# Mask read-back of a fused sparse-attention and FFN kernel: four SP transfers to 32 partitions, or two Pool transfers to 128

## The chip, the cores and the metric

The kernel runs on one core of a Trainium2 chip. The metric is the device time of one execution in microseconds, the median of several runs. Engines are named as in the profile: PE (TensorE), PEld (its weight loads), DVE (VectorE), ACT (ScalarE), POOL (GpSimd) and SP (SyncE, which here only issues DMAs). Each of SP and POOL feeds a DMA queue of its own; both queues are served by the same 16 DMA engines.

## The reference

Two operations in a row. First, attention over 4 sequences ("batches"), 8 heads, 768 positions and 64 channels, in which each query sees only 6 chunks of 32 keys; then a feed-forward block on the result.

```
k_min, k_max = min, max of each chunk of 32 keys
ub     = sum over channels of max(q * k_min, q * k_max)     # bound per query and chunk
ub     = -1e9 where the chunk lies in the query's future
sel    = the 6 chunks with the highest ub, for each query
scores = q k^T / 8, -1e9 where not (selected and key <= query)
x      = softmax(scores) v                                   # [3072, 512]
out    = relu(x w_in)^2 w_out                                # 512 -> 2048 -> 512
```

## The kernel before

The work is cut into 16 head pairs (4 batches of 4 pairs) and 5 FFN blocks. The first 128 queries of every sequence can see only the first four chunks, so they need no selection: they are computed first for all batches, and are the first FFN block. The other 640 queries (5 tiles of 128) of each batch follow, batch by batch, and each batch is an FFN block when its attention result `x` is complete.

For batches 0 and 1 the selection goes into the score product itself: 24 extra rows of the matmul operands add a large negative number where a chunk isn't selected. For batches 2 and 3 (the last two sequences, pairs 8 to 15) it goes another way, in `stage_a_turned`:

1. Keys and queries come turned, by DMA transposes on SP (`kt`, `qt`). DVE reduces the keys to chunk maxima and minima (`kr`, two reductions a pair, L666), halves the queries (`qp`, `qm`, L688), PE computes the bounds (`ub`, L656 and L658), DVE masks them (`ubm`, L680), finds the highest eight (`m`, MAX8, L651) and writes ones and zeros, scaled to a huge number and zero, into `selb` (L785).
2. SP turns `selb` by a DMA transpose into `sT` and writes that to a buffer in device memory, `seen` (L802).
3. SP reads `seen` back into `mask`, [128 keys, 2 heads, 20 units, 128 queries], repeating each row of `seen` for the 32 keys of its chunk (L806). A unit is a pair of a query tile and a key tile. `seen` holds 4 groups of 40 rows, one group for each chunk within a key tile, so four DMAs are issued, one for each group of 32 partitions, 328 kB each.
4. POOL makes the five diagonal blocks of the mask causal (`mask<-mask`, L835, five instructions a pair).
5. In `stage_b_turned`, PE computes scores (`ps`, L913), ACT the exponentials (`e`, L951), DVE takes the minimum of `e` and `mask` (L953, ten instructions a pair), PE multiplies by the values (`av`, L946), and DVE normalises into `x` (reciprocal L638, product L640).

The mask buffers come from a pool of two (`set`), which the extra-row operands of the first two batches use before them. So a pair's mask can be fetched only when the pair two before it has had its last minimum.

An FFN block needs `x` turned; for batches 1 to 3 that is five DMA transposes on SP (`xT<-x`, L414). PE's `ph` (L1009) is the first FFN product, ACT or DVE apply the ReLU (`ht`, L1016 and L1018), DVE squares (`h`, L1027), PE's `py` (L1040) is the second product, ACT copies it to `ob` (L300), and SP stores it (L1053).

The order of instructions on every engine is written by a planner, `Plan`, before anything runs. Each operation has its candidate engines with a cost, a due time, needs and tiles; `Plan.order` starts, on the engine that is free first, the operation with the earliest due time. Due times come from a table of fitted numbers, `P`: `lead` (how far ahead each pair's selection is due), `due` and `rate` (the FFN blocks), `loads` and `later` (the order of loads), `shift` (changes to single operations) and some more. DMAs are costed by `packets`, through a small model of the two queues, `Transfers`. An operation with `packets` and without `turns` is a load on POOL; loads keep a given order among themselves:

```
if op.packets and not op.turns and op is not self.loads[len(landed)]:
    continue
```

Once planned, each engine runs its instructions in that order, and a DMA's wait holds up all that its issuing engine has behind it.

Of the kernel before, what the change touches and what calls it, by code (L numbers as in the profile page):

```python
# [81 lines left out]
class Plan:  # L82
# [19 lines left out]
        self.loads = []  # L102

    def op(self, where, due, fn, needs=(), tiles=(), packets=0, turns=False,
           late=0.0, rows=128):
        op = Op(where, due, fn, [n for n in needs if n is not None],
                [t for t in tiles if t is not None], packets, turns)
        for t in op.tiles:
            t.users.append(op)
        op.late = late  # L110
        op.rows = rows
        op.number = -1 if packets and not turns else len(self.ops) - len(self.loads)
        self.ops.append(op)
        if packets and not turns:
            self.loads.append(op)
        return op

    def order(self):
        free = {e: 0.7 for e in ("PE", "ACT", "DVE", "POOL", "SP")}
        slots = {tag: [(0.0, i) for i in range(n)] for tag, n in self.slots.items()}  # L120
        waiting = {}
        count = {}
        for op in self.ops:
            for t in op.tiles:
                t.left = len(t.users)
            count[op] = len(op.needs)
            for n in op.needs:
                waiting.setdefault(n, []).append(op)
        ready = [op for op in self.ops if not count[op]]
        landed, done = [], []  # L130
        rows = 128
        dma = Transfers()
        while ready:
            found = []
            for op in ready:
                if op.packets and not op.turns and op is not self.loads[len(landed)]:
                    continue
                at = 0.0
                new = {}
                for t in op.tiles:  # L140
                    if not t.held:
                        new[t.tag] = new.get(t.tag, 0) + 1
                for tag, n in new.items():
                    at = max(at, sorted(slots[tag])[n - 1][0]
                             if n <= len(slots[tag]) else self.NEVER)
                if at == self.NEVER:
                    continue
                if op.packets and not op.turns and len(landed) >= 8:
                    at = max(at, landed[-8].end)
                for engine, cost in op.where.items():  # L150
                    st = max(at, free[engine])
                    for n in op.needs:
                        same = n.engine == engine and not n.packets
                        lag = (0.0 if engine == "PE" else self.BUSY) if same                             else self.HAND_OVER[n.engine]
                        st = max(st, n.end + lag)
                    for t in op.tiles:
                        if t.psum:
                            for e, end in t.last.items():
                                if e != engine and "PE" not in (e, engine):
                                    st = max(st, end + self.HAND_OVER[e])  # L160
                    found.append((st, op, engine, cost))
            assert found, "nothing can start"
            first = min(found, key=lambda f: (f[0], f[1].number))
            st, op, engine, cost = min(
                (f for f in found if f[2] == first[2] and f[0] <= first[0] + self.wait),
                key=lambda f: (round(f[1].due, 6), f[0], f[1].number))
            ready.remove(op)
            if engine == "PE":
                op.fill = 0
                fresh = [t for t in op.tiles if t.psum]  # L170
                if st < self.FILL and fresh and not any(t.held for t in fresh):
                    room = max([free[engine]] + [min(slots[t.tag])[0] for t in fresh])
                    op.fill = max(0, int((st - room - 0.3) / 0.216))
                if st < self.WARM:
                    cost *= 2
                if op.rows != rows:
                    cost += self.SWITCH
                rows = op.rows
            op.engine, op.start, op.end = engine, st, st + cost
            free[engine] = op.end  # L180
            if op.packets:
                dma.add(op)
                if not op.turns:
                    landed.append(op)
            for t in op.tiles:
                if not t.held:
                    t.held = True
                    slot = min(slots[t.tag])
                    slots[t.tag].remove(slot)
                    t.slot = slot[1]  # L190
                t.last[engine] = max(t.last.get(engine, 0.0), op.end)
                t.left -= 1
                if not t.left:
                    slots[t.tag].append(
                        (max(u.end + self.HAND_OVER[u.engine] for u in t.users),
                         t.slot))
            for n in waiting.get(op, ()):
                count[n] -= 1
                if not count[n]:
                    ready.append(n)  # L200
            done.append(op)
        assert len(done) == len(self.ops), "operations left"
        return sorted(done, key=lambda op: op.start)
# [12 lines left out]
def kernel(  # L216
# [9 lines left out]
    nc = tc.nc  # L226
# [17 lines left out]
    QC = 128 * NS  # L244
    VW = 80
    NSET = 4
    P = dict(lead=[-23.68, 210.01, 152.21, 144.05, -31.58, 102.41, 35.34, 55.13,
             115.99, 34.19, 31.08, 95.55, 110.01, 67.89, 4.75, 130.36], f_due=[381.13,
             -1344.18, -1072.84, -487.16], sp='K0 Q0 K1 Q1', rows=[-2152.97, -1713.16,
             -252.64, -1284.21, 1259.55, -368.8, -2131.49, -296.06], after=1,  # L250
             up_due=-58.884, up_rate=11.985, half=4, due=[-23.83, -165.81, -133.7,
             266.6], rate=[4.21, 8.73, 10.38, 24.63], va=22.291, vm=16.1, ra=-3.615,
             h2=-15.315, later='q1 k1 v1 k2 q2 v3 q3 v2 k3', shift={522: 9.76, 1364:
# [9 lines left out]
             1171: -9.73, 528: -4.83, 1419: -7.53, 1620: 4.17}, p0=-4855.279,  # L263
             wait=0.012, xt=(1, 2, 3), ub='ff', tp=1, vm2=3.232, va2=7.671,
             loads='V1 V0 Q3 K3 Q2 K2 i0 V2 k0 V3 q0 i1 k1 v2 q1 i2 v0 '
             'i3 k2 q2 o0 v1 o2 o1 k3 o3 v3 q3')

    nc.scalar.preload_act_table_set("natural_log_exp_and_others")

# [482 lines left out]
    NU = len(UNITS)  # L752
# [3 lines left out]
    written, placed = [], []  # L756

    def stage_a_turned(p):
        b, hp = divmod(p, NP)
        s = p % NSET  # L760
        t0 = HALVES * p - P["lead"][p]
        op = plan.op
        kT, qT = turned["k", b], turned["q", b]
        qp, qm = buffer("qp", [128, QC]), buffer("qm", [128, QC])
        ub = buffer(P["ub"], [128, NS, 2, NC], F32, name="ub")
        sT = buffer("st", [128, 2, 128], name="sT")
        seen = buffer("seen", [2 * 128, 128], name="seen")
# [23 lines left out]
        def pick(i0, i1):  # L791
            for i in range(i0, i1):
# [5 lines left out]
               for i, n in ((0, 3), (3, 2))]  # L798
# [4 lines left out]
            out=seen.tile.rearrange("(x r) j -> r x j", r=128), in_=sT.tile),  # L803
            [t] + written[-1:], [sT, seen], packets=300, turns=True, late=1.0)
        written.append(w)
        spread = [op({"SP": 0.45}, t0 + 25 + g, lambda _, g=g: nc.sync.dma_start(  # L806
            out=mask[32 * g:32 * g + 32].rearrange("c h u j -> c (h u j)"),
            in_=seen[2 * NU * g:2 * NU * (g + 1)].rearrange(
                "r j -> (r j)").unsqueeze(0).to_broadcast([32, 2 * NU * 128])),
            [w] + placed[-1:], [seen, mask], packets=930, turns=True, late=0.5) for g in range(4)]  # L810
        placed.append(spread[0])
        prepared[p, "mask"] = [op({"POOL": 0.37}, t0 + 30 + t, lambda _, t=t:
                                  causal("POOL", mask[:, :, FIRST[t] + t + 1], 2),
# [247 lines left out]
    for b in range(B):  # L1061
        due = P["f_due"][b]
# [18 lines left out]
    for b in range(B):  # L1081
# [28 lines left out]
        if last:  # L1110
            down(NS - 1, 0, 384)
            down(NS - 1, 384)
    computed = [op for op in plan.ops if op.turns or not op.packets]
    for i, change in P["shift"].items():
        computed[i].due += change
    with tc.manual_schedule():
# [31 lines left out]
```

## Time and profile before

| | |
|---|---|
| median of 3 runs | 274.06 us (273.2 to 274.55) |
| profiled execution | 274.56 us, span 272.7 us, granted clock 0.987 |
| PE, PEld busy | 252.5 us (93%), 159.1 us (58%) |
| DVE, ACT, POOL busy | 203.5, 181.6, 111.3 us (75, 67, 41%) |
| POOL queue | 75088 packets, 13.11 MB, 64.1% of 16 engines |
| SP queue | 33904 packets, 23.73 MB, 41.4% of 16 engines |
| mask read-back | 32 DMAs of 320 KB, median 5.9 us from issue to landing |

A row of a timeline reads: start, duration (us), engine, line, operation, output<-input, count, and in brackets the idle time of that engine before it and what ended it. A row of the chain reads: start, duration, engine, tile, line, count. In rows of groups, the numbers behind the bar are busy us, mean ns of one, and idle time before with what ended it. KB there is 1024 bytes.

### The profile page before, as it was taken

How to read it: one execution, taken by the hardware profiler on the slowest of the kernel's cores; microseconds unless marked ns; L12 is line 12 of the kernel's file. 1: busy time of each engine (PE TensorE's matmuls, PEld its weight loads, DVE VectorE, ACT ScalarE, POOL GpSimd, SP SyncE). 2: the span in 40 equal slices, each digit the busy share in tenths (PEclk: the TensorE clock that was granted, in tenths of full speed). 3: DMA queues.
4: the chain of work that ended last, by engine and by line, in shares of the span. 5: the costliest groups of instructions: out<-in, count | busy, mean ns of one | idle time of the engine just before them, and what ended most of it. 6: DMA issues, size and time to landing. Idle time of an engine off the chain costs nothing.

```text
span 272.7 us, 6942 instructions
## 1 busy us (share of the span) xinstructions
PE 252.5 (93%) x2519; PEld 159.1 (58%) x2543; DVE 203.5 (75%) x760; ACT 181.6 (67%) x361; POOL 111.3 (41%) x186
## 2 busy tenths in 40 slices
PE   7888999999999999997699989986999999999995
PEld 2566466656677556663486645543776654775443
DVE  7449999887999999994489999986989840355000
ACT  6767898747996988983287745774887741487111
POOL 7979887799179685620303030432003400000000
PEclk9999999999999999999599999999999999999999
DMA  9999999999999999969694829779497025100022
GB/s 157 153 173 159 174 192 189 98 160 199 125 126 183 135 176 144 103 129 191 132 252 83 199 52 229 181 196 198 127 216 151 0 60 154 77 2 0 38 79 78
DMA packets 109026, 37.29 MB, mean 137 GB/s; under 512 B 100672, under 2 KB 105024, under 8 KB 107968
## 3 DMA queue, kind: packets, MB, share of 16 engines
q0 software_dynamic: 75088, 13.11, 64.1%
q1 hardware_dynamic: 33904, 23.73, 41.4%
q8 instruction: 20, 0.33, 0.5%
q14 instruction: 14, 0.11, 0.2%
HBM read 37.75 MB, written 6.82 MB: 163 GB/s over the span
## 4 chain that ended last, share of the span: by engine, by line
PE 46%; DVE 34%; DMA 9%; POOL 5%; issue 2%; ACT 1%; SPq 0%; DVEq 0%; POOLq 0%; ACTq 0%
PE py L1040 19%; PE ph L1009 17%; DVE kr L666 7%; DVE h L1027 5%; DMA xT<-x 4%; DVE selb L785 4%; DVE m L651 3%; DVE ht L1018 3%; DVE e L953 3%; PE ps L855 3%; DMA mask<-seen 3%; DMA qn<-in_q_dram 2%; PE av L946 2%; PE av L867 2%; PE ps L913 2%
## 5 line engine op out<-in xcount | busy, mean ns | idle before, releaser
L1009 PE MATMUL ph<-xT,w_in_sb 128*128 128x256 bf16 (+2 forms) x592 | 97.3, 307 | 8.5 <-DMA xT<-x 5.9
L1040 PE MATMUL py<-w_out_sb,h 128*128 128x512 bf16 (+2 forms) x376 | 89.1, 372 | 2.2 <-DVE ubm L680 0.7
L1009 PEld LDWEIGHTS <-w_in_sb 128*128 128x128 bf16 x592 | 55.5, 98 | 35.4 <-DMA xT<-x 6.5
L1016 ACT ACTIVATE ht<-ph 128x384 bf16<-128x384 f32 (+2 forms) x115 | 52.2, 455 | 26.8 <-PE ph L1009 21.3
L1027 DVE TENSOR_TENSOR h<-ht 128x256 bf16<-128x256 bf16 (+2 forms) x148 | 48.0, 336 | 12.0 <-ACT ht L1016 9.4
L1040 PEld LDWEIGHTS <-h 128*128 128x128 bf16 x400 | 35.9, 98 | 34.8 <-issue 1.5
L835 POOL TENSOR_SCALAR_AFFINE_SELECT mask<-mask 128x256 bf16<-128x256 bf16 x40 | 19.1, 514 | 76.8 <-DMA mask<-seen 45.8
L951 ACT ACTIVATE e<-ps 128x512 bf16<-128x512 f32 x80 | 42.9, 603 | 9.9 <-PE ps L913 9.2
L879 ACT ACTIVATE e<-ps 128x512 bf16<-128x512 f32 x80 | 43.5, 611 | 4.5 <-PE ps L855 4.1
L300 ACT COPY ob<-py 128x512 f32<-128x512 f32 (+2 forms) x25 | 14.2, 569 | 37.7 <-PE py L1040 37.3
L953 DVE TENSOR_TENSOR e<-e,mask 128x512 bf16<-128x512 bf16 x80 | 33.0, 437 | 7.5 <-POOL mask L835 6.8
L1018 DVE TENSOR_SCALAR ht<-ph 128x256 bf16<-128x256 f32 (+2 forms) x33 | 15.9, 481 | 15.2 <-PE ph L1009 15.1
L855 PE MATMUL ps<-kqc 88*128 88x128 bf16 (+2 forms) x160 | 25.9, 272 | 0.4
L835 POOL TENSOR_SCALAR_AFFINE_SELECT e<-e 128x128 bf16<-128x128 bf16 (+1 forms) x50 | 17.3, 360 | 16.5 <-ACT e L879 16.3
L946 PEld LDWEIGHTS <-e 128*128 128x128 bf16 x320 | 15.4, 100 | 9.1 <-DVE e L953 2.2
L640 DVE TENSOR_TENSOR x<-av,rc 128x320 bf16<-128x320 f32 (+1 forms) x40 | 18.4, 469 | 0.3
L946 PE MATMUL av<-vn,e 128*128 128x65 bf16 x240 | 17.9, 196 | 0.4 <-DVE e L953 0.2
L855 PEld LDWEIGHTS <-kqc 88*128 88x128 bf16 x160 | 13.6, 97 | 7.3 <-issue 1.1
L867 PEld LDWEIGHTS <-e 128*128 128x128 bf16 x320 | 13.8, 97 | 3.3 <-POOL e L835 0.3
L651 DVE MAX8 m<-ubm 128x8 f32<-128x24 f32 x160 | 15.2, 164 | 0.1
L666 DVE TENSOR_REDUCE kr<-kt 128x24 bf16<-128x768 bf16 x16 | 14.8, 938 | 0.0
L666 DVE TENSOR_REDUCE kr<-kT 128x24 bf16<-128x768 bf16 x16 | 14.8, 948 | 0.1
(96 smaller groups left out, 312.4 us busy)
## 6 DMA issues: line engine op xcount, KB each, us to landing
mask<-seen SPq DMA_DIRECT2D x32, 320.0 KB, 5.9
out_dram<-ob SPq DMA_DIRECT2D x23, 256.0 KB, 3.2
w_in_sb<-in_moe_w_in_dram POOLq DMA_DIRECT2D x4, 512.0 KB, 7.7
w_out_sb<-in_moe_w_out_dram POOLq DMA_DIRECT2D x4, 512.0 KB, 8.5
vn<-in_v_dram POOLq DMA_DIRECT2D x15, 128.0 KB, 6.1
nt<-in_k_dram POOLq DMA_DIRECT2D x10, 128.0 KB, 7.5
nt<-in_q_dram POOLq DMA_DIRECT2D x10, 128.0 KB, 6.6
kn<-in_k_dram POOLq DMA_DIRECT2D x8, 80.0 KB, 7.3
```

The costliest lines, as they stand in the source:

```text
L666: nc.vector.tensor_reduce(split(kr[:, mm]), by_chunk(view(kT)), axis=AX.X, op=f), got, [kT, kr])
L835: nc.gpsimd.affine_select(out=e, in_=e, compare_op=ALU.is_ge, fill=0.0, base=0, channel_multiplier=-1, pattern=[[0, n], [1, 128]])
L855: nc.tensor.matmul(ps[:, 128 * c:128 * (c + nt)], lhsT=kqs(slice(0, KC), s, hh)[:, 128 * j:128 * (j + 1)], rhs=qss(slice(0, KC), s, hh)[:, ...
L879: nc.scalar.activation(e.tile, ps.tile, ACT.Exp, scale=scale), [sc], [ps, e])
L946: nc.tensor.matmul(av[:, t - 1], lhsT=e[:, 128 * c:128 * (c + 1)], rhs=value_tile(b, h, j), start=(i == 0 and c == 0), stop=(i == NB - 1), ...
L951: done = plan.op({"ACT": 0.48}, due + 0.5, lambda _: nc.scalar.activation(e.tile, ps.tile, ACT.Exp, scale=scale), [sc], [ps, e])
L953: done = plan.op({"DVE": 0.335}, due + P["vm2"], lambda _: nc.vector.tensor_tensor(e.tile, e.tile, masks[p][:, hh, 4 * i:4 * i + 4].rearrange(
L1009: nc.tensor.matmul(ph.tile, lhsT=w_in_sb[:, ki, 128 * f:128 * (f + 1)], rhs=xT[:, c0 // 128:c1 // 128, ki], start=(ki == 0), stop=(ki == N ...
L1016: nc.scalar.activation(ht.tile, ph.tile, ACT.Relu)
L1018: nc.vector.tensor_scalar_max(ht.tile, ph.tile, 0.0)
L1027: {"DVE": 0.067 + w / 1920}, at[0] + P["h2"], lambda _: nc.vector.tensor_mul(h2[f][:, c0:c1], ht.tile, ht.tile), [op], [ht, h2[f]])))
L1040: nc.tensor.matmul(py.tile, lhsT=h2[f][:, 128 * t:128 * (t + 1)], rhs=w_out_sb[:, f, c0:c1], start=(f == 0), stop=(f == NFI - 1))
```

## The change

The read-back of the mask moves from SP to POOL and is cut by head instead of by group of partitions: two DMAs a pair, each for one head and all 128 partitions, 655 kB each. The source is viewed as 4 groups, each repeated 32 times. The new DMAs are marked `free`: they aren't in the loads' fixed order, but count as transfers of POOL's queue. The table `P` is fitted anew, so the order of instructions changes on every engine; in `later`, batch 3's keys now stand before its queries.

```
     def op(self, where, due, fn, needs=(), tiles=(), packets=0, turns=False,
-           late=0.0, rows=128):
+           late=0.0, rows=128, free=False):
...
-        op.number = -1 if packets and not turns else len(self.ops) - len(self.loads)
+        op.load = bool(packets) and not turns and not free
+        op.number = -1 if op.load else len(self.ops) - len(self.loads)
...
-                if op.packets and not op.turns and op is not self.loads[len(landed)]:
+                if op.load and op is not self.loads[loads]:
                     continue
...
                 if not op.turns:
                     landed.append(op)
+                    loads += op.load
...
-    P = dict(lead=[-23.68, 210.01, 152.21, 144.05, -31.58, 102.41, 35.34, 55.13,
+    P = dict(lead=[-18.56, 229.84, 152.55, 102.48, -28.79, 99.16, 39.06, 55.0, 124.03,
...
-             h2=-15.315, later='q1 k1 v1 k2 q2 v3 q3 v2 k3', shift={522: 9.76, 1364:
+             h2=-3.478, later='q1 k1 v1 k2 v3 q2 k3 v2 q3', shift={1461: -2.33, 615:
...
-             loads='V1 V0 Q3 K3 Q2 K2 i0 V2 k0 V3 q0 i1 k1 v2 q1 i2 v0 '
-             'i3 k2 q2 o0 v1 o2 o1 k3 o3 v3 q3')
+             loads='V0 K3 Q2 V1 K2 Q3 i0 V2 k0 V3 q0 i1 k1 v2 q1 i2 v0 '
+             'i3 k2 q2 o0 v1 o2 k3 o1 o3 v3 q3')
...
-        spread = [op({"SP": 0.45}, t0 + 25 + g, lambda _, g=g: nc.sync.dma_start(
-            out=mask[32 * g:32 * g + 32].rearrange("c h u j -> c (h u j)"),
-            in_=seen[2 * NU * g:2 * NU * (g + 1)].rearrange(
-                "r j -> (r j)").unsqueeze(0).to_broadcast([32, 2 * NU * 128])),
-            [w] + placed[-1:], [seen, mask], packets=930, turns=True, late=0.5) for g in range(4)]
+
+        def spread_rows(hh):
+            rows = seen[0:8 * NU].rearrange("(g h u) j -> g h (u j)", g=4, h=2)
+            nc.gpsimd.dma_start(
+                out=mask[:, hh].rearrange("c u j -> c (u j)"),
+                in_=rows[:, hh].unsqueeze(1).to_broadcast([4, 32, NU * 128]))
+
+        spread = [op({"POOL": 0.80}, t0 + 25 + hh, lambda _, hh=hh: spread_rows(hh),
+                     [w] + placed[-1:], [seen, mask], packets=2000, free=True, late=0.3)
+                  for hh in range(2)]
```

In the order that the planner writes now, SP has 32 DMAs fewer and POOL 16 more. POOL has nothing of batches 0 and 1 left when the first of them is reached; from there on its instructions are the mask DMAs and the forty causal selects alone.

More of the change, by code (lines that the diff above doesn't have):

```diff
@@ L111, in op @@
         op.rows = rows
-        op.number = -1 if packets and not turns else len(self.ops) - len(self.loads)
+        op.load = bool(packets) and not turns and not free
+        op.number = -1 if op.load else len(self.ops) - len(self.loads)
         self.ops.append(op)
-        if packets and not turns:
+        if op.load:
             self.loads.append(op)
@@ L129, in order @@
         ready = [op for op in self.ops if not count[op]]
-        landed, done = [], []
+        landed, done, loads = [], [], 0
         rows = 128
@@ L246 @@
     NSET = 4
-    P = dict(lead=[-23.68, 210.01, 152.21, 144.05, -31.58, 102.41, 35.34, 55.13,
[L248 to L252, printed above, removed]
-             h2=-15.315, later='q1 k1 v1 k2 q2 v3 q3 v2 k3', shift={522: 9.76, 1364:
[9 rows of a table removed]
-             1171: -9.73, 528: -4.83, 1419: -7.53, 1620: 4.17}, p0=-4855.279,
-             wait=0.012, xt=(1, 2, 3), ub='ff', tp=1, vm2=3.232, va2=7.671,
-             loads='V1 V0 Q3 K3 Q2 K2 i0 V2 k0 V3 q0 i1 k1 v2 q1 i2 v0 '
-             'i3 k2 q2 o0 v1 o2 o1 k3 o3 v3 q3')
+    P = dict(lead=[-18.56, 229.84, 152.55, 102.48, -28.79, 99.16, 39.06, 55.0, 124.03,
+             40.34, 7.99, 96.78, 112.44, 66.15, 16.87, 125.31], f_due=[-61.33,
+             -1388.83, -1240.75, -707.33], sp='K0 Q0 K1 Q1', rows=[-1131.22, -1431.25,
+             109.16, 501.8, -517.91, 1199.14, -3841.51, 427.48], after=1,
+             up_due=-63.179, up_rate=9.427, half=4, due=[-24.24, -119.06, -171.27,
+             87.42], rate=[4.2, 9.11, 10.54, 36.48], va=15.226, vm=4.436, ra=2.591,
+             h2=-3.478, later='q1 k1 v1 k2 v3 q2 k3 v2 q3', shift={1461: -2.33, 615:
[9 rows of a table added]
+             -10.62, 1597: 9.23, 1075: 10.49, 1343: -1.75}, p0=-9815.44, wait=0.009,
+             xt=(1, 2, 3), ub='ff', tp=1, vm2=6.919, va2=10.415,
+             loads='V0 K3 Q2 V1 K2 Q3 i0 V2 k0 V3 q0 i1 k1 v2 q1 i2 v0 '
+             'i3 k2 q2 o0 v1 o2 k3 o1 o3 v3 q3')
     nc.scalar.preload_act_table_set("natural_log_exp_and_others")
@@ L1112 @@
             down(NS - 1, 384)
-    computed = [op for op in plan.ops if op.turns or not op.packets]
+    computed = [op for op in plan.ops if not op.load]
     for i, change in P["shift"].items():
```

18 rows, old and new, of the table h2 are left out of this document.

## The prediction

> **What bounds the kernel now.** I read the page's busy shares and its chain that ended last, then that chain in order of time around the change, the waits, each queue's timeline there, and the busy time by stage. The time is 274.56 us for the profiled execution, whose span is 272.7 us; 1.9 us lie outside the span. The median of the three runs is 274.06 us, so a sum made on 274.56 loses 0.5 us at the end.
>
> ```profile
> PE 252.5 (93%) x2519; PEld 159.1 (58%) x2543; DVE 203.5 (75%) x760; ACT 181.6 (67%) x361; POOL 111.3 (41%) x186
> ```
> ```profile
> 125.50 6.04 DMA xT<-x
> 131.59 1.03 PE ph L1009 x4
> ...
> 173.39 6.88 DMA mask<-seen
> 180.57 0.41 POOL mask L835
> ...
> 181.53 1.45 DVE e L953 x3
> ...
> 183.98 5.64 DMA xT<-x
> 189.76 0.60 PE ph L1009 x4
> 190.48 0.86 PE py L1040 x4
> ```
>
> PE has little air: 272.7 - 252.5 = 20.2 us. A change can give back only what PE loses, so I look where that is. The chain shows two transposes by DMA, of batch 1's and batch 2's attention result (`xT<-x`), and a mask between them.
>
> ```profile
> 120.00:136.00 16.00, 12.00 (x114) 6.66 (x116) 8.54 (x44) 6.14 (x13) 2.21 (x5) 0.81 0.87 152
> 136.00:152.00 16.00, 15.80 (x154) 11.08 (x152) 15.26 (x45) 12.51 (x29) 2.25 (x5) 0.97 0.67 167
> 152.00:168.00 16.00, 14.46 (x172) 8.88 (x173) 16.00 (x81) 8.55 (x18) 2.15 (x5) 1.00 0.69 151
> 168.00:184.00 16.00, 14.60 (x196) 8.35 (x197) 14.35 (x49) 11.58 (x23) 5.41 (x10) 1.00 0.79 194
> 184.00:200.00 16.00, 13.66 (x196) 9.85 (x195) 12.86 (x56) 10.59 (x25) 1.84 (x5) 1.00 0.82 171
> 131.60:136.20 4.60, 4.38 (x29) 2.89 (x31) 2.45 (x8) 1.72 (x4) 1.13 (x3) 0.50 0.51 104
> ```
>
> The columns are the stretch, its length, busy time of PE, PEld, DVE, ACT, POOL, then the granted clock, DMA share and GB/s. PE is idle 4.0 us in the first stage, 0.2 + 1.5 + 1.4 in the next three, 2.3 in the fifth: 9.5 us in all. The last line is the second bill for the first stop: after it PE runs at half clock for 4.6 us, 2.3 us lost. DVE is full from 136 to 168, and idle just before:
>
> ```profile
> 131.59 1.03 PE L1009 MATMUL ph<-xT,w_in_sb 128*128 128x256 bf16 x4 [3.69 <-DMA xT<-x]
> ```
> ```profile
> 130.97 1.14 DVE L953 TENSOR_TENSOR e<-e,mask 128x512 bf16<-128x512 bf16 x2 [5.24 <-POOL mask L835]
> ```
> ```profile
> 120.88 1.98 SPq L806 DMA_DIRECT2D mask<-seen  x4
> 122.96 1.17 SPq L414 DMA_TRANSPOSE sT<-selb  x1
> 124.22 8.35 SPq L414 DMA_TRANSPOSE xT<-x  x5
> 180.58 2.07 SPq L806 DMA_DIRECT2D mask<-seen  x4
> 182.75 6.90 SPq L414 DMA_TRANSPOSE xT<-x  x5
> 222.63 2.50 SPq L414 DMA_TRANSPOSE xT<-x  x2
> ```
>
> This is the mechanism. Each time four mask DMAs go out on SP's queue, the five transposes that PE wants next are issued right behind them: 1.67 us each (8.35 / 5) and 1.38 (6.90 / 5), against 1.25 (2.50 / 2) where no mask is ahead. Their landing suffers too:
>
> ```profile
> DMA to landing us min/median/max: 2.4/2.7/6.8
> ```
> ```profile
> DMA to landing us min/median/max: 3.7/5.9/10.4
> ```
>
> The first line is `xT`, the second `mask`. PE's first FFN block needs two transposes. Without a mask ahead the second would be issued at 124.22 + 1.25 and land 2.7 later, at 128.2, not 131.5.
>
> **The change: the mask transfers.** 32 issues leave SP, 16 come to POOL; 10.5 MB move either way. What a transfer of the new form costs the trace does not show; two stretches bound it.
>
> ```profile
> 198.00:209.00 11.00, 11.00 (x134) 7.36 (x132) 9.80 (x30) 8.68 (x20) 2.22 (x5) 1.00 1.02 214
> 253.00:273.00 20.00, 16.41 (x92) 8.23 (x90) 0.07 (x1) 3.08 (x6) 0.00 (x0) 1.00 0.18 67
> ```
>
> From 198 to 209 only masks are on the move, into 32 partitions each: 214 GB/s with the engines full (share 1.02). From 253 on only results leave, from all 128 partitions: 67 GB/s at a share of 0.18, 372 GB/s at a share of 1. A DMA of 655 kB thus takes 1.8 us at the better rate and 3.1 at today's. I take 1.8, since the new form spans 128 partitions as those do, and keep 3.1 for the range. [...]
>
> ```profile
> L459 POOL DMA_DIRECT2D nt<-in_q_dram x10 | 9.0, 903 | 3.2 <-DMA qt<-nt 1.1 <-DMA kt<-nt 1.1 <-issue 0.9
> L835 POOL TENSOR_SCALAR_AFFINE_SELECT mask<-mask 128x256 bf16<-128x256 bf16 x40 | 19.1, 514 | 76.8 <-DMA mask<-seen 45.8 <-DVE h L1027 9.5 <-DVE selb L785 9.5
> 130.53 2.21 POOL L835 TENSOR_SCALAR_AFFINE_SELECT mask<-mask 128x256 bf16<-128x256 bf16 x5 [11.79 <-DMA mask<-seen]
> ```
>
> Issue: POOL pays 0.90 us a DMA (load row), 16 x 0.90 = 14.4 us. It is idle 76.8 us ahead of the mask selects, so the bill itself is hidden. Landing: a lone mask DMA took at least 3.7, of which 1.5 are its 328 kB at 214 GB/s, so 2.2 us are fixed. A pair lands 2 x 0.90 + 1.8 + 2.2 = 5.8 us after POOL starts (9.1 if 3.1 each, the first one's transfer partly behind the second's issue). Now it is 130.53 - 120.88 = 9.65 us from the first issue to the selects.
>
> **The first stop (3.7 + 2.3 us).** The masks no longer stand ahead of `xT` on SP, and by the order of instructions POOL sends the first pair right after its last select of batch 1 (130.53 - 11.79 = 118.7 now), well before 124. PE's cover grows too: between batch 1's last value product and the first FFN product there are now 24 `py` products, two bursts of `ps` and ten bounds, in the new order 36, two and ten. At 0.86 us for four `py` that is 2.6 us more. With the last value product about 1.5 us of PE work earlier in the new order, PE arrives at 127.9 + 2.6 - 1.5 = 129.0, after 128.2. The 3.69 us go, and with them the reason for the half clock: -6.0 us.
>
> **DVE behind it (2 us).** The refit loads batch 3's keys before its queries. Of the eight key reductions that stand behind batch 1's last normalisation now, two go ahead of it, and six between it and the first `min` with a mask (none now). By the count of DVE's order that normalisation comes no later, since other work has left the stretch.
>
> ```profile
> L666 DVE TENSOR_REDUCE kr<-kt 128x24 bf16<-128x768 bf16 x16 | 14.8, 938 | 0.0
> 141.29 0.94 DVE kr L666
> 143.37 0.86 DVE kr L666
> 145.18 0.86 DVE kr L666
> 146.44 0.86 DVE kr L666
> 149.56 0.53 DVE kr L666
> 157.16 0.85 DVE kr L666
> ```
>
> The six pieces of the chain, 4.9 us, stand where DVE is full today; moved ahead, they fill the 5.24 us of idleness. Against that stand new waits: POOL works in order, and the fifth mask's DMAs (waiting for the third's buffer) stand ahead of the fourth's five selects, the sixth's ahead of the fifth's. From that release POOL needs 2 x 0.90 + 2.2 = 4.0 us. DVE, counted in the new order (two query halves, two normalisations, one bound and ten MAX8; the second time ten selections and two normalisations), has about 2.6 and 2.4 us to do: 1.4 and 1.6 lost, 3.0 in all. Net -2, between -3.1 (all of PE's idleness from 136 to 184) and +1.
>
> **The second stop (2.2 us).** In the new order the sixth mask's two DMAs still go just before `xT`, so part of the collision stays; cover grows from 20 `py` to 28, 1.7 us. PE now waits 5.9 - 3.7 = 2.2 us there:
>
> ```profile
> DVE e L953 <- POOL mask L835: 6.8, 4, 5.2
> ...
> PE ph L1009 <- DMA xT<-x: 5.9, 2, 3.7
> ```
>
> I take -1.6, between 0 and -2.2. The third `xT` loses cover, 60 `py` to 44, but 44 are 9.5 us and two transposes 1.25 + 2.7: nothing. A few copies go from DVE to ACT (some 2 us): nothing, since ACT has 3.5 us or more to spare in each 16.
>
> Sum: 274.56 - 6.0 - 2.0 - 1.6 = 265.0, on the median 264.5; half a microsecond for small waits of the new order makes 265.0. Own range: 262.5 (all 9.5 + 2.3 of idleness and half clock gone) to 270 (transfers at 3.1, stop two unchanged, +1 on DVE).
>
> **Rivals.** (1) *Four engines.* The new source is four groups of rows, each repeated 32 times. If a transfer is dealt out by those four groups, four of the 16 DMA engines carry 164 kB each: 7.0 us at 372 / 16 = 23 GB/s, 12.3 at 214 / 16 = 13.4. [...] The two DMAs run beside each other on different engines. At 7.0 the pair lands 1.8 + 7.0 + 2.2 = 11 us after POOL starts, 13.2 with the selects, against the 12 us or so that DVE's order leaves between the release and the first `min` of the fourth to sixth mask: 1 to 1.6 us for each of three, 4.5 in all: 269.5. At 12.3 it is 18.5 us: 5 to 7 us too late for masks one, four, five and six, some 24, of which PE's FFN work hides about 10: 279, slower than before. It decides from about 10 us a transfer. For it: the form; against the slow end: 13.4 GB/s is seen only for 32 partitions.
>
> (2) *Pool in order.* If not two but all eight masks cost 1.5 us of waiting, as at the two places above, 9 us more are lost: 274, no change. For it: POOL now holds DMAs, waits and selects in one queue. Against: at the other six places the order leaves DVE 5 us or more.
>
> **Chances.** Forecast 0.50; four engines at the quick rate 0.15 (269.5), at the slow rate 0.20 (279); Pool in order 0.15 (274; 0.04 faster, 0.07 same, 0.04 slower). Half a per cent, 1.4 us, is about what a measurement of this kernel can tell from no change. Faster 0.50 + 0.15 + 0.04 = 0.69, same 0.07, slower 0.24. The range runs from 262 (the forecast's low end) to 276, leaving out the slow four engines.
>
> **What the profile after would show.** Right: PE never idle over 1.5 us before `ph`, clock 1.00 from 120 to 136, `xT` issues of 1.25 us, mask landing under 5 us by the median, DMA rate in mask stretches above 300 GB/s or share well under 1. Wrong: mask landing of 8 us or more, DVE waiting for POOL's selects by more than 6.8 us in total, or a PE stop ahead of `xT` that is still there though the masks landed early.

## The result and the profile after

The changed kernel takes 325.22 us (323.81 to 328.36, median of 4 runs), the kernel before, beside it, 273.64 us (273.2 to 274.55): a ratio of 1.190, 95% interval 1.180 to 1.200. The forecast was 265.0, with a range of 262 to 276. The profiled execution took 324.14 us, its span is 322.4 us. Medians and ranges here and below are of all executions; ratios and their intervals leave out those more than 1.5% above the quickest of the same kernel.

The page of after, from its busy shares, its slices, its chain by line and its DMA issues:

```profile
PE 262.8 (82%) x2545; PEld 164.0 (51%) x2545; DVE 205.2 (64%) x754; ACT 183.3 (57%) x368; POOL 120.6 (37%) x201
...
PEclk9599999999999999659958995976956999999999
...
DMA mask<-seen 15%; PE py L1047 14%; DMA sT<-selb 10%; PE ph L1016 9%; DVE kr L668 6%; DMA seen<-sT 6%; DMA nt<-in_q_dram 4%; DMA qn<-in_q_dram 2%; DMA qt<-nt 2%; DVE m L653 2%; DVE h L1034 2%; DVE selb L787 2%; DVE e L960 2%; DMA xT<-x 2%; DVE x L642 1%
...
mask<-seen POOLq DMA_DIRECT2D x16, 640.0 KB, 15.9
```

The span grew by 322.4 - 272.7 = 49.7 us. PE was idle for 20.2 us and is now for 322.4 - 262.8 = 59.6: 39.4 of the 49.7. The other 10.3 are PE being busy for longer (262.8 against 252.5) at the same work; the clock line shows why, slices down to half speed between 129 and 250 us, around PE's stops. Three DMA steps, which were no large part of the chain before, now hold 31% of it: the mask, the transpose of the selection (`sT`) and its way to device memory (`seen`). A mask DMA lands 15.9 us after its issue by the median, not 5.9.

The same stages as in the prediction, and one more (columns as there):

```profile
120.00:136.00 16.00, 8.83 (x76) 4.09 (x74) 9.53 (x32) 4.42 (x9) 0.00 (x0) 0.85 1.30 92
136.00:152.00 16.00, 12.65 (x122) 9.63 (x123) 10.78 (x45) 8.14 (x21) 3.19 (x7) 0.73 0.80 159
152.00:168.00 16.00, 8.08 (x73) 4.58 (x71) 8.49 (x38) 6.41 (x13) 3.34 (x7) 0.81 0.38 62
168.00:184.00 16.00, 15.35 (x170) 8.61 (x168) 13.89 (x69) 9.73 (x19) 3.50 (x7) 0.87 0.39 104
184.00:200.00 16.00, 6.94 (x90) 4.06 (x91) 6.27 (x26) 4.54 (x9) 3.67 (x7) 0.77 0.82 119
...
232.00:248.00 16.00, 7.62 (x70) 5.51 (x71) 7.54 (x22) 3.87 (x9) 5.03 (x9) 0.57 0.40 102
```

PE works about half the time in four of the six, and DVE no longer fills any of them. From 152 to 168 the DMA share is 0.38 while PE is busy for 8.08 of 16 us: the DMA engines are mostly idle while PE, at the end of a chain of waits, stands still for DMAs. A transfer that only a few engines carry would look like that; the experiments count them.

The waits of after, and the chain of waits in order of time from the first mask on:

```profile
POOL mask L842 <- DMA mask<-seen: 71.1, 6, 19.1
...
DVE e L960 <- POOL mask L842: 37.9, 6, 10.9
POOL mask L811 <- DMA seen<-sT: 37.8, 3, 20.2
...
PE av L953 <- DVE e L960: 34.2, 6, 9.8
```
```profile
133.92 5.22 DMA xT<-x
139.27 5.13 PE ph L1016 x24
144.41 17.76 DMA sT<-selb
162.18 1.65 DMA seen<-sT
163.89 0.47 issue
164.38 0.67 POOL mask L811
165.05 1.99 POOL mask L842 x5
167.04 11.08 DMA mask<-seen
...
183.91 13.44 DMA sT<-selb
197.37 16.49 DMA seen<-sT
...
215.27 21.71 DMA mask<-seen
```

The fourth row of waits is the end of a line: PE waits 34.2 us for minima, these wait 37.9 for selects, these 71.1 for masks. The chain shows the part that no step of the prediction had. A transpose of `sT` takes 17.76 and 13.44 us from its issue to its landing, its write to `seen` took 16.49 once, and only then can the next mask start, which loads the same DMA engines again. Masks were under way each time: those issued from 142.83 on landed at 162.1 and 162.5, where the first of these transposes lands at 162.18; those from 186.03 on landed at 213.6 and 214.4, where the write lands at 213.86. Mask, transpose and write hold each other up in turn. By the median, from the DMA views of before and of after:

```profile
sT<-selb SPq DMA_TRANSPOSE x8, 3.8
```
```profile
sT<-selb SPq DMA_TRANSPOSE x8, 14.2
```

The first mask's pair, in POOL's timeline, and what SP did meanwhile:

```profile
117.53 1.41 POOL L811 DMA_DIRECT2D mask<-seen  x2
137.74 1.84 POOL L842 TENSOR_SCALAR_AFFINE_SELECT mask<-mask 128x256 bf16<-128x256 bf16 x5 [18.80 <-DMA mask<-seen]
```
```profile
122.27 10.29 SPq L416 DMA_TRANSPOSE sT<-selb  x1
132.65 7.71 SPq L416 DMA_TRANSPOSE xT<-x  x5
```

The pair goes out at 117.53, and its selects start at 137.74. SP meanwhile needs 10.29 us for the issue of a single transpose, 1.17 in before, and `xT` begins 8 us later than before. PE stops 10.44 us there.

### The profile page after: what moved, and what is told of

Same layout as the page of the kernel before. It is cut to its first block, busy times and chain, and to the rows that moved or that the text cites. A ratio compares the mean times of both kernels' runs of the same rounds, so it can differ in the third digit from the quotient of the medians.

```text
span 322.4 us, 6946 instructions
## 1 busy us (share of the span) xinstructions
PE 262.8 (82%) x2545; PEld 164.0 (51%) x2545; DVE 205.2 (64%) x754; ACT 183.3 (57%) x368; POOL 120.6 (37%) x201
## 4 chain that ended last, share of the span: by engine, by line
DMA 40%; PE 27%; DVE 20%; POOL 7%; issue 2%; SPq 1%; ACT 1%; POOLq 0%; DVEq 0%; ACTq 0%
DMA mask<-seen 15%; PE py L1047 14%; DMA sT<-selb 10%; PE ph L1016 9%; DVE kr L668 6%; DMA seen<-sT 6%; DMA nt<-in_q_dram 4%; DMA qn<-in_q_dram 2%; DMA qt<-nt 2%; DVE m L653 2%; DVE h L1034 2%; DVE selb L787 2%; DVE e L960 2%; DMA xT<-x 2%; DVE x L642 1%
## 5 line engine op out<-in xcount | busy, mean ns | idle before, releaser
L1016 PE MATMUL ph<-xT,w_in_sb 128*128 128x256 bf16 (+2 forms) x592 | 102.4, 319 | 15.4 <-DMA xT<-x 10.4
L1047 PE MATMUL py<-w_out_sb,h 128*128 128x512 bf16 (+2 forms) x400 | 93.4, 377 | 0.0
L1023 ACT ACTIVATE ht<-ph 128x384 bf16<-128x384 f32 (+2 forms) x118 | 53.6, 459 | 51.1 <-PE ph L1016 36.7
L1016 PEld LDWEIGHTS <-w_in_sb 128*128 128x128 bf16 x592 | 57.6, 102 | 43.8 <-DMA xT<-x 10.9
L960 DVE TENSOR_TENSOR e<-e,mask 128x512 bf16<-128x512 bf16 x80 | 35.2, 475 | 40.3 <-POOL mask L842 37.9
L958 ACT ACTIVATE e<-ps 128x512 bf16<-128x512 f32 x80 | 43.2, 601 | 28.2 <-PE av L953 11.6
L842 POOL TENSOR_SCALAR_AFFINE_SELECT mask<-mask 128x256 bf16<-128x256 bf16 x40 | 17.7, 478 | 71.1 <-DMA mask<-seen 71.1
L953 PE MATMUL av<-v,e 128*128 128x65 bf16 x80 | 13.6, 214 | 34.7 <-DVE e L960 33.8
L953 PEld LDWEIGHTS <-e 128*128 128x128 bf16 x320 | 16.3, 107 | 44.6 <-DVE e L960 39.8
L811 POOL DMA_DIRECT2D mask<-seen x16 | 10.8, 679 | 46.0 <-DMA seen<-sT 37.8
L862 PE MATMUL ps<-kqc 88*128 88x384 bf16 (+2 forms) x160 | 26.1, 272 | 0.5 <-DVE ubm L682 0.3
L1025 DVE TENSOR_SCALAR ht<-ph 128x256 bf16<-128x256 f32 (+2 forms) x30 | 14.1, 469 | 13.2 <-PE ph L1016 12.9
L842 POOL TENSOR_SCALAR_AFFINE_SELECT e<-e 128x128 bf16<-128x128 bf16 (+1 forms) x48 | 16.8, 366 | 9.8 <-ACT e L886 8.6
L874 PEld LDWEIGHTS <-e 128*128 128x128 bf16 x320 | 14.2, 97 | 4.0 <-POOL e L842 0.9
## 6 DMA issues: line engine op xcount, KB each, us to landing
mask<-seen POOLq DMA_DIRECT2D x16, 640.0 KB, 15.9
```

The costliest lines, as they stand in the source:

```text
L842: nc.gpsimd.affine_select(out=e, in_=e, compare_op=ALU.is_ge, fill=0.0, base=0, channel_multiplier=-1, pattern=[[0, n], [1, 128]])
L862: nc.tensor.matmul(ps[:, 128 * c:128 * (c + nt)], lhsT=kqs(slice(0, KC), s, hh)[:, 128 * j:128 * (j + 1)], rhs=qss(slice(0, KC), s, hh)[:, ...
L953: nc.tensor.matmul(av[:, t - 1], lhsT=e[:, 128 * c:128 * (c + 1)], rhs=value_tile(b, h, j), start=(i == 0 and c == 0), stop=(i == NB - 1), ...
L958: done = plan.op({"ACT": 0.48}, due + 0.5, lambda _: nc.scalar.activation(e.tile, ps.tile, ACT.Exp, scale=scale), [sc], [ps, e])
L960: done = plan.op({"DVE": 0.335}, due + P["vm2"], lambda _: nc.vector.tensor_tensor(e.tile, e.tile, masks[p][:, hh, 4 * i:4 * i + 4].rearrange(
L1016: nc.tensor.matmul(ph.tile, lhsT=w_in_sb[:, ki, 128 * f:128 * (f + 1)], rhs=xT[:, c0 // 128:c1 // 128, ki], start=(ki == 0), stop=(ki == N ...
```

## The experiments

Runs of one set shared their runs of before (274.79 us beside the first four, 274.55 beside the next four, 274.19 beside the last three, in the order below). All but one start from after, and so have its order of instructions.

**The form of the source, at POOL, in four steps.** First, after with the four DMAs of before, issued by POOL:

```
-            nc.gpsimd.dma_start(
-                out=mask[:, hh].rearrange("c u j -> c (u j)"),
-                in_=rows[:, hh].unsqueeze(1).to_broadcast([4, 32, NU * 128]))
+            for g in (2 * hh, 2 * hh + 1):
+                nc.gpsimd.dma_start(
+                    out=mask[32 * g:32 * g + 32].rearrange("c h u j -> c (h u j)"),
+                    in_=seen[2 * NU * g:2 * NU * (g + 1)].rearrange(
+                        "r j -> (r j)").unsqueeze(0).to_broadcast([32, 2 * NU * 128]))
```

> Order of instructions as in the changed kernel, mask still on POOL's queue, but in the form of before: each of the two operations issues two DMAs to 32 partitions with one group of rows repeated 32 times. Theory A (the new form's outermost source dimension of 4 puts each DMA on four of the 16 engines): mask landing falls from a median of 15.9 us to 6 to 8 us, the DMA share in mask stretches goes back to about 1, the time falls to 266 to 276 us. Rival B (POOL's queue is slow at repeated reads, whatever the form): landing stays above 12 us and the time above 310. Rival C (the refitted order is what costs): landing is short and the time still above 300.

Measured: 273.71 us (271.1 to 278.16), ratio 0.993 (0.988 to 0.998). Theory A held. The 51.5 us are gone with the form alone; queue and order stay. Its mask issues, its SP timeline at the first stop, PE's restart there, and three waits:

```profile
mask<-seen POOLq DMA_DIRECT2D x32, 320.0 KB, 6.1
```
```profile
123.16 10.84 SPq L416 DMA_TRANSPOSE xT<-x  x5
```
```profile
133.75 5.49 PE L1017 MATMUL ph<-xT,w_in_sb 128*128 128x256 bf16 x28 [4.60 <-DMA xT<-x]
```
```profile
POOL mask L811 <- DMA seen<-sT: 10.3, 2, 6.5
...
PE ph L1017 <- DMA xT<-x: 4.9, 2, 4.6
...
DVE e L961 <- POOL mask L843: 3.5, 1, 3.5
```

Though SP has no mask on its queue, its five transposes take 10.84 us to issue, longer than behind the masks (8.35), and PE stops 4.60 us.

Next, two DMAs to 128 partitions as in after, but `seen` is written in copies, so that the source has 16 rows with 8 repeats each, or 8 rows with 16:

```
+                nc.sync.dma_start(
+                    out=to[g], in_=sT[64 * (g % 2):64 * (g % 2) + 64, g // 2].unsqueeze(
+                        1).to_broadcast([64, 4, 128]))
...
-                in_=rows[:, hh].unsqueeze(1).to_broadcast([4, 32, NU * 128]))
+                in_=rows.unsqueeze(1).to_broadcast([4 * 4, 32 // 4, NU * 128]))
```

> As the changed kernel, two POOL DMAs a pair to 128 partitions, but the write of seen leaves four copies of each group in device memory (four SP DMAs of 64 rows instead of one), so that the source's outermost dimension is 16 with 8 repeats, not 4 with 32. A: 16 engines work, landing 4 to 6 us, 1.8 to 3.1 us of transfer a DMA, time 264 to 272 us, at or below e1. B: landing above 12 us, time above 310. C: short landing, time above 300.

> As e2 with two copies: outermost dimension 8 with 16 repeats. A: eight engines, landing between e2's and the changed kernel's, 7 to 11 us, time 268 to 290 us. B: as the changed kernel, 315 to 330. C: above 300.

Measured: 282.94 us (281.01 to 283.3), ratio 1.029 (1.021 to 1.036), with 16; 302.52 us, ratio 1.103 (1.093 to 1.112), with 8. Mask issues with 16 rows, then with 8:

```profile
mask<-seen POOLq DMA_DIRECT2D x16, 640.0 KB, 6.6
```
```profile
mask<-seen POOLq DMA_DIRECT2D x16, 640.0 KB, 10.4
```

Destination, bytes and queue are those of after; the landing goes 15.9, 10.4, 6.6 us for 4, 8 and 16 rows in the slowest dimension. In the packet records of the first pair, the counts of packets under way that hold longest are 4 and 8 with 4 rows, 8 and 16 with 8, and 16 with 16, as one or both of its transfers run. Read as engines, these counts give a transfer as many as its source has rows there: 4, 8 and 16. With 16, a pair of 1.31 MB still took 6.35 us by its packets, 206 GB/s and no more than in the old form. Theory A thus had the engines right, and with 8 rows the landing too; with 16 it had 4 to 6 us for 6.6. Both its times (264 to 272 and 268 to 290 us) were missed. The waits and the chain give a likely cause: the four writes of copies make `seen` late, 33.0 us of waiting against 10.3, and the chain of the run with 16 rows holds `seen` for 7% and `sT` for 5%, where that of the run above lists neither.

```profile
POOL mask L819 <- DMA seen<-sT: 33.0, 3, 14.0
```

**The queue.** Before, in its own order, with the new form issued by SP; then after, with the old form issued by SP (as the first diff, with `nc.sync`):

```
-            out=mask[32 * g:32 * g + 32].rearrange("c h u j -> c (h u j)"),
...
+            nc.sync.dma_start(
+                out=mask[:, hh].rearrange("c u j -> c (u j)"),
+                in_=rows[:, hh].unsqueeze(1).to_broadcast([4, 32, NU * 128]))
```

> Before's parameters and order, mask on SP, but in the new form: two DMAs a pair, four groups repeated 32 times, 128 partitions. A: the form alone is slow: landing above 12 us, at least as slow as on POOL since both DMAs of a pair may use the same four engines, time above 300 us. B: 268 to 280 us, since SP's queue is not POOL's. C: 268 to 280 us, since the order is that of before.

> The new order of instructions, but the masks issued by SP in the form of before (four DMAs of 32 partitions, two at each of the two places). Theory Q (the choice of queue hardly matters once all 16 engines serve the mask, since both queues share them): time within 1.5% of the POOL variant e1, 270 to 278 us, and the xT issues stretched as there (above 1.5 us each). Rival (SP's order is what held xT up): xT lands later than in e1 and the time is 4 us or more above it.

Measured: 340.0 us, ratio 1.239 (1.228 to 1.251), and 272.32 us (270.14 to 273.47), ratio 0.991 (0.987 to 0.995). Theory A held in the first: the new form is as bad on SP, without the refit and without POOL's queue (its waits):

```profile
POOL mask L841 <- DMA mask<-seen: 140.4, 8, 25.8
...
DVE e L959 <- POOL mask L841: 52.1, 7, 12.1
```

The old form on SP, in its PE timeline at the first stop and in its waits:

```profile
131.43 5.02 PE L1017 MATMUL ph<-xT,w_in_sb 128*128 128x256 bf16 x28 [2.38 <-DMA xT<-x]
```
```profile
PE ph L1017 <- DMA xT<-x: 5.6, 2, 3.3
```

It is no slower than the same order with the masks on POOL, and its `xT` issues are stretched too, 7.58 / 5 = 1.52 us at the first stop: for the old form, the queue does not decide the time.

The new form on SP gives the clearest count. By its packet records a lone pair takes 14.7 to 15.1 us, each packet of 5120 bytes 0.20 us by the median, and four packets are under way at nearly every moment. So, by this count, the two DMAs of a pair share four engines. Nor is a packet slow for being read 32 times: 0.20 us is what one with a row of its own takes (below). Too few are under way. On POOL's queue, in after, it is five to seven on average, eight for about a third of the time: the second DMA partly runs beside the first, and still a lone pair needs 11.8 to 20.3 us, with packets of 0.28 to 0.44 us by the mean. Why a pair has four engines on SP and up to eight on POOL was not shown: the trace does not number the engines.

**The load by itself.** The run with the old form on POOL, with a quarter of the mask's bytes (the rest of the mask is left out); and after, with its four-engine DMAs, but nobody waits for them (minima read a constant tile, the causal selects are left out):

```
-            e.tile, e.tile, masks[p][:, hh, 4 * i:4 * i + 4].rearrange(
+            e.tile, e.tile, masks[p][:, 0, 0:4].rearrange(       # a quarter
+            e.tile, e.tile, opened, op=ALU.min),                 # nobody waits
```

> As e1, but each mask DMA moves a quarter of its bytes, and selects and minima read that quarter (most of the mask is left out, so the results mean nothing). Theory D (mask bytes on the shared engines hold up xT and all else; the order itself is as good as forecast): first PE stop ahead of xT under 1.5 us, no half clock after it, time 262 to 267 us. Rival (the order has stops of its own): time stays within 1% of e1, 271 to 276 us.

> As the changed kernel, its four-engine mask DMAs included, but nobody waits for them: the minima read a constant tile, and POOL's causal selects are left out (no mask is applied). Theory L (waiting for the mask's landing is the loss): time falls to 265 to 278 us. Rival H (the four loaded engines hold up the transfers of all others, above all the transposes and the writes of seen on SP, which need every engine): the landing of sT stays above 10 us, PE still stops ahead of xT for more than 5 us, and the time stays above 285 us.

Measured: 266.25 us, ratio 0.969 (0.962 to 0.976), and 296.59 us, ratio 1.080 (1.071 to 1.089): theory D held, and rival H. With a quarter of the bytes the first stages are what the prediction promised, PE and DVE full, the clock at 1.00:

```profile
120.00:136.00 16.00, 15.29 (x147) 9.63 (x146) 15.90 (x61) 9.43 (x22) 3.98 (x9) 1.00 0.61 125
136.00:152.00 16.00, 15.47 (x187) 10.10 (x186) 15.42 (x70) 12.59 (x28) 7.41 (x13) 1.00 0.28 74
```

With nobody waiting for masks, 296.59 - 274.55 = 22.0 us of loss remain. They come from SP's transposes, in the waits (5.9 us for `xT` before), the chain and the DMA view:

```profile
PE ph L1016 <- DMA xT<-x: 29.7, 3, 13.6
```
```profile
201.66 21.68 DMA xT<-x
```
```profile
sT<-selb SPq DMA_TRANSPOSE x8, 16.8
```

So some 22 us of the loss are engines held for others, and the rest, 325.2 - 296.6 = 28.6 by difference, is waiting for the masks themselves. The split isn't exact, since with nobody waiting the masks' DMAs are issued at other times.

**What limits the rate.** After with 128 distinct source rows (a tile written once beforehand; the flags are not read, so nothing waits for them); the 16 rows with another pitch; and distinct rows in the old form, 32 partitions a DMA:

```
+                in_=wide[:, NU * 128 * hh:NU * 128 * (hh + 1)])        # 128 distinct rows
-            rows = seen.tile.rearrange("(n r) j -> n (r j)", r=64)[
+            rows = seen.tile.rearrange("(n r) j -> n (r j)", r=68)[    # other pitch
+                    in_=wide[32 * g:32 * g + 32])                       # 32 partitions, distinct
```

> As the changed kernel, but the mask's source is 128 different rows in device memory, not four groups repeated 32 times (the values are not the mask's; one extra 1.3 MB write is made once ahead). All 16 engines by its form. Theory S (reading the same few rows over and over limits the rate to the 206 to 222 GB/s seen so far): a pair's transfer takes 3.5 to 4.5 us, above 290 GB/s. Rival T (these transfers run at some 210 GB/s whatever they read): 6 us or more a pair.

> e2_sixteen_rows with its sixteen copies of the flags 68 rows of 256 bytes apart in DRAM instead of 64; same bytes, same partitions, same issues. There a pair of mask transfers of 1.31 MB took 6.35 us, 206 GB/s, where e8_no_repeats, which reads 128 distinct rows, needed 4.3 to 4.7 us. Theory pitch: sixteen source rows that begin at multiples of 16 KB share something in the memory, and with another pitch a pair takes 4.8 us or less, the mask's packets about 0.20 us each and the time falls by 2 to 5 us from 282.9. Rival, repeats: reading each row eight times is what limits, whatever the pitch: a pair stays at 6.0 to 6.6 us and the time at 281 to 284.

> The four mask transfers of the kernel before, 32 partitions each, on POOL's queue in the order of after, but each of the 128 partitions reads a row of its own (a tile written once beforehand, so that the flags are not read at all: this part of the computation is left out, and nothing waits for the flags). Differs from e8_no_repeats in the partitions of one transfer alone, from e1_pool_old_form in the repeated source alone (there a pair took 6.5 us, a packet of 10240 bytes 0.65 to 0.80 us). Theory partitions: 32 partitions are what keeps the old form slow, so a pair takes 6 to 6.6 us as in e1 and the median landing stays near 6. Rival, repeats: a pair takes 4.3 to 4.9 us as in e8, a packet about 0.4 us, and the median landing is 5 or less. Time by the first 270 to 274, by the second 267 to 271.

Measured, one run each: 269.49, 280.67 and 283.04 us. By the packet records:

| destination | source | packet, median | pair, undisturbed |
|---|---|---|---|
| 128 partitions | 128 distinct rows | 0.196 us for 5120 B | 4.3 to 4.7 us |
| 128 partitions | 16 rows, 8 times each | 0.27 to 0.39 us for 5120 B | 6.2 to 6.4 us |
| 128 partitions | the same, other pitch | 0.28 to 0.38 us for 5120 B | 5.8 to 6.3 us |
| 32 partitions | 128 distinct rows | 0.66 to 0.79 us for 10240 B | 6.5 to 7.0 us |
| 32 partitions | one row, 32 times | 0.63 to 0.79 us for 10240 B | 6.5 to 7.3 us |

With distinct rows theory S held but for 0.2 us at its upper end: a pair moves at 282 to 303 GB/s. Pitch makes little difference; its rival held within 0.4 us. In the third run the theory of partitions held for the transfers, and both theories missed the time (270 to 274 and 267 to 271). That run isn't explained: its first pair took 11.6 us (10.0 with the repeated rows), and PE's waits for `xT` sum to 8.6 us (4.9 with the repeated rows), from transfers of the same bytes and length. Two costs of like size stand here. With 32 partitions a byte costs twice what it costs with 128 and distinct rows by the median packet, and half again as much by the whole pair, whatever the source; with 128 partitions, repeated rows cost nearly as much, 6.2 to 6.4 us a pair. The second cost was seen with 16 rows and sixteen packets under way, and not with four rows read 32 times each by four engines on SP, where a packet took 0.20 us and a pair moved at 87 to 89 GB/s. For the first, the median packets come to a factor of two, 0.78 against 2 x 0.196 us; the pairs, 6.5 to 7.0 against 4.3 to 4.7, show less. What causes it was not shown. By these runs, the change did away with the first cost and would have met the second, had it got its sixteen engines.

PE's restart at the first stop, with 128 partitions and distinct rows:

```profile
132.21 3.96 PE L1023 MATMUL ph<-xT,w_in_sb 128*128 128x256 bf16 x28 [3.01 <-DMA xT<-x]
```

**The order by itself.** The order of after with the masks in their old form on SP, once more:

> The kernel of e5_sp_old_form once more, with more rounds: the order of after, the four mask transfers of the kernel before on SP. There the ratio was 0.9911 with 0.9868 to 0.9954. Theory refit: the order alone is worth 2 to 3 us, the ratio is 0.989 to 0.994 and its interval stays below 0.9975. Rival, chance: the kernel is the same as before within its spread, and the interval holds 1.

Measured: 272.26 us (269.23 to 273.95, 6 runs) beside 274.19. The ratio, 0.985 (0.977 to 0.992), is that of the three quickest; the medians of all runs give 0.993 here and 0.992 in the first series. Both intervals stay below 1, so the refitted order is worth something from 0.7 to 1.5%. By the median it is the quickest kernel of this study that leaves nothing out, though 273.71 with the masks on POOL is within its spread. Its first stop, with the same program as in the first series:

```profile
132.28 5.38 PE L1017 MATMUL ph<-xT,w_in_sb 128*128 128x256 bf16 x28 [4.76 <-DMA xT<-x]
```

It was 2.38 us there: a single profile does not fix the length of this stop.

## Why the prediction was wrong, point by point

- **The price of a mask transfer: wrong, and decisive.** "I take 1.8, since the new form spans 128 partitions as those do." The row it came from stores results, and each of its bytes leaves from a place of its own. The new form reads four rows 32 times, and so gets four engines (four packets under way on SP, four or eight in after): on SP a lone pair moved for 14.7 to 15.1 us, in after for 11.8 to 20.3, where the price was 1.8 a DMA. Even with sixteen (the run with 16 rows) a DMA takes 6.35 / 2 = 3.2 us: the bound of 3.1, not the value taken. With distinct rows it takes 2.2 to 2.3, so no run reached 1.8.
- **Rival 1, four engines: the right mechanism, with 0.35 of the chance, and the wrong time.** Its quick rate was good: 23 GB/s an engine forecast, 5120 B / 0.20 us = 26 measured on SP. "The two DMAs run beside each other on different engines" was wrong on SP and half true on POOL, so the first pair landed some 20 us after POOL started, not the 11 of the quick rate; by the slow rate it would have been 1.8 + 12.3 + 2.2 = 16.3. Above all it billed lateness only where minima wait for masks, 4.5 to 24 us less what FFN work hides. It gave no price to the other transfers on those engines: 22 us where nobody waits for masks, and with the waits a ring from mask to `sT` to `seen` to the next mask. "13.4 GB/s is seen only for 32 partitions" weighed a rate where the load on others mattered.
- **The first stop, -6.0: the reason failed.** "The masks no longer stand ahead of `xT` on SP" is true and did not remove the stop. With the masks on POOL in the old form, at a DMA share of 1.15 from 120 to 136, `xT` still went out at 10.84 / 5 = 2.17 us an issue (1.25 forecast) and PE stopped 4.60 us; with the masks on SP in the same order it stopped 2.38 and, in the second series, 4.76, so the queue makes no clear difference here. With distinct rows, a transfer close to the price forecast, it still stopped 3.01 us, though its page has the clock at 0.9 or more in every slice from there on. Without three quarters of the bytes the stop is gone: no wait of PE for `xT` is left, where all bytes leave 4.9 us. The transposes collide with the masks' bytes on the DMA engines, more than with their place in a queue.
- **DVE, -2.0: borne out where the masks are in time.** DVE is busy for 15.90 of the 16 us from 120 on with a quarter of the bytes, where it had a gap of 5.24. The waits that the prediction added, 1.4 + 1.6, show in the old form on POOL as one of 3.5. There is no sign of rival 2, "Pool in order", in that run.
- **The second stop, -1.6: right on one queue, wrong on the other.** With the old form on POOL the two waits for `xT` sum to 4.9, of which the first is 4.6, so 0.3 are left of 2.2. With the old form on SP, in the same order of instructions, it is 3.3 and 3.0, longer than before: here the masks do stand right ahead of `xT` on the queue.
- **The sum.** The kernel that the steps described, all engines and short masks, is nearest to the run with a quarter of the bytes, 266.25 us, and to that with distinct rows, 269.49 (one run); both leave part of the mask's work out. Of the 9.6 us forecast, 8.3 and 5.1 are there. So the arithmetic for the order was sound where the bytes are few, and 265.0 rested on a transfer of 1.8 us that no run gave.
- **What would show it.** The signs of "wrong" came: landing 15.9 (limit 8) and DVE waiting 37.9 us for selects (limit 6.8). But they would have been read as late masks only, and some 22 us of the loss are not that.

## What to carry to other kernels

Before two broadcast reads replace four, look at the slowest dimension of the source: with 4 there, a transfer got 4 engines here, and a median landing of 5.9 us became one of 15.9. Price such a transfer by what else uses those engines, above all by DMA transposes in the same chain, and only then by who waits for its data. A refitted order and a new transfer should be run apart: here the one was worth -1% and the other +19%.

## What the runs showed of the hardware that was not expected

- Transfers on four engines held up others on another queue: `sT`'s median landing went from 3.8 to 14.2 us, to 16.8 where nobody waited for the masks, and a transpose's issue on SP once took 10.29 us.
- Reading 16 rows 8 times each was slower than reading 128 distinct rows: 0.27 to 0.39 us for 5120 bytes against 0.196, with 128 partitions in both. Another distance between the rows left it so. Four engines on four rows showed nothing of it on SP, 0.20 us. Whether the memory or the DMA engines' reads cause it stays open.
- PE's stops cost twice here: of the 49.7 us, 10.3 are PE's own work at a lower granted clock, 0.57 to 0.87 from 136 to 248 us in the rows shown.
